# A gated mix of a Fourier layer and a Mish layer: the hand-ordered step list becomes a list of operations that a planner orders

## The chip, the cores and the metric

The kernel runs on one core of one Trainium2 chip. The metric is the device time of one execution in microseconds (us), the median of the runs shown; lower is better. The engines are TensorE (PE in the profile, PEld for its weight loads), VectorE (DVE), ScalarE (ACT), GpSimd (POOL) and SyncE (SP), which here issues nearly all DMAs. Each engine works through its own list in order.

## The reference

`x` is 2048 x 640 (S x D), and F is 1728. Two branches are mixed by a gate per row:

```python
g = sigmoid((x * gate_w).sum(-1, keepdims=True))
a, b = x @ Wd_re.T, x @ Wd_im.T                 # 640 x 640 each
y = Ws_re @ a - Ws_im @ b                       # 2048 x 2048 each
h = x @ w1 + b1
z = (h * tanh(softplus(h))) @ w2                # Mish; 640 x 1728 x 640
out = g * y + (1 - g) * z
```

All numbers are float32. The matrices of the Fourier branch are inputs; the kernel treats them as any matrices.

## The kernel before, in words

**Precision.** Every operand of a matmul is held as two numbers, a high part (the value copied to the type `fp32r`) and a low part (value less high part). A block product is three matmuls of 128 x 128 by 128 x 512: high x high, high x low, low x high (`mm3`). Making an operand (`split`, L82) costs one copy on ACT and one subtraction on DVE.

**Three products in turn.** The transposed result is made in three stages, of the kinds `seq` (the sequence products, with x as weights, kh = 8), `hid` (the hidden products, kh = 5) and `out` (the product with w2, kh = 6); the dense layer with w1 and Mish stands between hid and out. Intermediate tiles u (after seq), y (after hid) and act (after Mish) go to DRAM and are read back.

**Sums for products.** Within a stage a `Problem` treats two row tiles t1 and t2 of 512 columns and two halves of the inner dimension at once, by a scheme of the Strassen and Winograd kind: seven products in place of eight over four of the five 128-wide column blocks of the weights, on sums and differences of the operands. The fifth column block (block 5, columns 512 to 640) is multiplied plainly. A `Problem` has three parts: `first` (L302), which multiplies the top half a11 and leaves partial sums in banks a (two) and d1; `second` (L343) with the operands 22, 21, s2 = a21 + a22 - a11 and s1 = a21 + a22; `third` (L409) with 12, s3 = a11 - a21 and s4. Operand 21 serves only bank d2, block 5 of t2. PSUM has eight banks, all of them in use inside a Problem. Partial sums that must wait are copied to SBUF, or, for four Problems whose first part runs early (`aside`), to DRAM.

**Weights.** For each k the stage makes weight tiles with their two parts: `XA` (top block, block 5, one sum), `XB`, `XT13` and `XT2`. The 26 slots of pool W hold them; seq alone needs 26, hid 16. At the last Problem of a stage XA[k] is freed after s1 of k, in `second`; XB and XT13 after s4 of k, in `third`.

**The dense stage.** `dense_rest` (L673) makes the last two blocks of h for one t (25 matmuls). `dense_first` (L734) makes the other twelve, a pair fp and fp + 6 in eight steps: a11, s1, d2, s2, s4 + d1, s3, a12 + d1, a22 + d2, 54 matmuls in all, on four banks. Between uses of a bank a snapshot is taken: `snap` (L789) copies bank a after a11, bank b after s1, bank a after s2. `w1_job` (L605) makes the weights of one fp: two loads, four sums, six splits.

**Gate.** A job per t (`gate`, L885) multiplies tiles of the transposed x by columns of gate_w and adds them up on DVE, sums over partitions by two matmuls with ones, takes the sigmoid and stores g and 1 - g as full tiles. `gate_y` (L919) later loads each of the 20 tiles of y, multiplies it by g and stores it again. 1 - g is multiplied into the results of the first out Problem (`done`, `give`) and into act for t = 2, 3 (`out_act`, `act_q`).

**Order.** The program is a list of steps of matmuls. For each step, operands are made LEAD = 7 steps ahead (6 in the dense stage), loads are issued up to AHEAD = 9 beyond that while enough buffers are free, stores three steps later. Weights, gates and multiplications are jobs in a fixed list, started when a running estimate of DVE's clock (`clock["dve"]`) lies behind PE's by a set slack, and not in the steps `quiet` around the start of the dense stage. All loads and all stores but one go through SP in this order.

Of the kernel before, what the change touches and what calls it, by code (L numbers as in the profile page):

```python
# [13 lines left out]
P = 128  # L14
# [8 lines left out]
LEAD = 7  # L23
LEAD_D = 6
AHEAD = 9
SPARE, SPARE_D, SPARE_OUT = 3, 5, 4
SLACK, SLACK_UP = -1.0, 2.5
NR, NFS, NFX, NW, NL = 10, 20, 4, 26, 4
MM = 0.2267


class Slots:


    def __init__(self, items):
        self.free = list(items)

    def get(self):
        return self.free.pop(0)

    def put(self, *items):
        self.free.extend(items)
# [3 lines left out]
def fnet_mish_gate(ctx: ExitStack, tc: tile.TileContext, xn, xt, c_re, c_im, wd_re, wd_im,  # L46
# [7 lines left out]
    psum = Slots([pp.tile([P, N], F32, name=f"ps{i}") for i in range(8)])  # L54
    R = Slots([(sb.tile([P, N], F32R, name=f"rh{i}"), sb.tile([P, N], F32R, name=f"rl{i}")) for i in range(NR)])
    FS = Slots([sb.tile([P, N], F32, name=f"f{i}") for i in range(NFS)])
    FX = Slots([sb.tile([P, D], F32, name=f"fx{i}") for i in range(NFX)])
    W = Slots([(sb.tile([P, D], F32R, name=f"wh{i}"), sb.tile([P, D], F32R, name=f"wl{i}")) for i in range(NW)])
    ones = sb.tile([P, P], F32R, name="ones")
    b1s = sb.tile([P, NF], F32, name="b1s")  # L60
    gws = sb.tile([P, KD], F32, name="gws")

    def scratch(name, n, rows=P):
        return [[dr.tile([rows, N], F32, name=f"{name}{i}_{t}") for t in range(TG)] for i in range(n)]

    usc, ysc = scratch("u", 2 * KD), scratch("y", KD)
    gsc, qsc = scratch("g", 1)[0], scratch("q", 1)[0]
    asc = scratch("act", FC) + [[dr.tile([FR, N], F32, name=f"actr_{t}") for t in range(TG)]]

    clock = {"pe": 0.0, "dve": 0.0, "step": 0}  # L70
# [4 lines left out]
    def tt(o, a, b, op):  # L75
        clock["dve"] += 0.14 + 0.54 * a.shape[-1] / N
        nc.vector.tensor_tensor(o, a, b, op=op)  # L77

    def copy(o, a, scale=1.0):
        nc.scalar.activation(o, a, AF.Copy, scale=scale)  # L80

    def split(h, l, src):  # L82

        copy(h, src)
        tt(l, src, f32(h), OP.subtract)

    def mm(ps, a, b, start, stop):
        clock["pe"] += MM
        nc.tensor.matmul(ps, a, b, start=start, stop=stop, skip_group_check=True)  # L89

    def mm3(ps, ah, al, bh, bl, start, stop):
        mm(ps, ah, bh, start, False)
        mm(ps, ah, bl, False, False)
        mm(ps, al, bh, False, stop)

    def part(w, a, b):
        return w[0][:, a:b], w[1][:, a:b]

    def blocks(w, at, n):
        return [part(w, at + j * P, at + (j + 1) * P) for j in range(n)]  # L100

    A2, B2 = slice(0, 2 * P), slice(2 * P, 4 * P)

    RAW, XS, PS, OPS, KEEP, X, H = {}, {}, {}, {}, {}, {}, {}
    steps, stores, events, attach, narrow, takes = [], [], {}, [], set(), {}

    def at(i, fn):

        events.setdefault(i, []).append(fn)

    def step(raw, preps, mms, post=None):
        steps.append([list(raw), list(preps), mms, post])

    def store(dst, v, f):
        stores.append((dst, v, f, clock["step"] + (3 if clock["step"] < len(steps) - 8 else 0)))


    jobs, loaded, running, done_jobs = [], [], [], set()  # L120

    class Job:
        def __init__(self, key, work, load=lambda: [], w=0, fx=0, fs=0):
            self.key, self.work, self.load, self.w, self.fx, self.fs = key, work, load, w, fx, fs

    def simple(fn):
        def work(*a):
            fn(*a)
            return
            yield  # L130
        return work

    def fx_load(src, width=D):
        f = FX.get()
        nc.sync.dma_start(f if width == D else f[:, :width], src)
        return f

    def fs_load(src):
        f = FS.get()
        nc.sync.dma_start(f[:src.shape[0]], src)  # L140
        return f

    def job_load(i):
        j = jobs.pop(0)
        loaded.append((j, j.load(), i))

    def job_start():
        j, a, _ = loaded.pop(0)
        running.append((j.key, j.work(*a)))

    def job_go():
        key, work = running[0]
        pause = next(work, None)
        if pause is None:
            running.pop()
            done_jobs.add(key)
        return pause or 0

    def need(key):
        while key not in done_jobs:  # L160
            if not running:
                if not loaded:
                    job_load(0)
                job_start()
            job_go()

    class Stage:  # L170


        def __init__(self, kind, kh, row, neg=False):
            self.kind, self.kh, self.row, self.neg = kind, kh, row, neg
            self.XA, self.XB, self.XT13 = [None] * kh, [None] * kh, [None] * kh
            self.XT2 = [None] * (kh // KD + 1)

    def t2_part(st, k):
        return part(st.XT2[k // KD], k % KD * P, (k % KD + 1) * P)

    def b_sums(f, g):

        t = FS.get()
        tt(f[:, A2], f[:, B2], f[:, A2], OP.subtract)
        tt(f[:, B2], g[:, B2], f[:, B2], OP.subtract)
        tt(t[:, A2], g[:, B2], f[:, A2], OP.subtract)
        tt(t[:, B2], g[:, A2], t[:, A2], OP.subtract)
        return t

    def top(st, k, a, five):  # L190
        w = st.XA[k] = st.XA[k] or W.get()
        split(*part(w, 0, 2 * P), a)
        split(*part(w, 2 * P, 3 * P), five)

    def low(st, k, g, f):
        if st.neg:
            copy(g, g, -1.0)
            yield 1
        t = b_sums(f, g)
        yield 0  # L200
        w = st.XB[k] = W.get()
        st.XA[k] = st.XA[k] or W.get()
        st.XT13[k] = W.get()
        if k % KD == 0:
            st.XT2[k // KD] = W.get()
        split(*w, g)
        FX.put(g)
        yield 0
        split(*part(st.XA[k], 3 * P, 5 * P), t[:, B2])
        split(*part(st.XT13[k], 4 * P, 5 * P), t[:, :P])  # L210
        split(*t2_part(st, k), t[:, P:2 * P])
        FS.put(t)
        yield 0
        split(*part(st.XT13[k], 0, 4 * P), f)
        FS.put(f)

    tops = set()

    def stage_jobs(st, order):
        def do_top(k, g):  # L220
            top(st, k, g[:, A2], g[:, 4 * P:])
            FX.put(g)

        for what, k in order:
            if what == "top":
                jobs.append(Job((st.kind, "top", k), simple(lambda g, k=k: do_top(k, g)),
                                lambda k=k: [fx_load(st.row(k))], (st.kind, k) not in tops, 1))
            else:
                jobs.append(Job((st.kind, "low", k), lambda g, f, k=k: low(st, k, g, f),
                                lambda k=k: [fx_load(st.row(k + st.kh)), fs_load(st.row(k)[:, :4 * P])],  # L230
                                2 + (k % KD == 0) + ((st.kind, k) not in tops), 1, 1))
            tops.add((st.kind, k))

    def c_split(key, f):
        r = OPS[key] = R.get()
        split(r[0], r[1], f)
        FS.put(f)

    def op_done(key):
        R.put(OPS.pop(key))  # L240

    def product(name, stationary, key, first, last):

        if first and name not in PS:
            PS[name] = [psum.get() for _ in stationary]
        for ps, w in zip(PS[name], stationary):
            mm3(ps, *w, *OPS[key], first, last)

    def products_by_part(uses, key):

        h, l = OPS[key]
        todo = []
        for name, stationary in uses:
            PS[name] = [psum.get() for _ in stationary]
            todo += zip(PS[name], stationary)
        for n, c in ((0, h), (0, l), (1, h)):
            for ps, w in todo:
                mm(ps, w[n], c, n == 0 and c is h, False)

    def free_banks(name):  # L260
        psum.put(*PS.pop(name))

    def copy_out(name, keep=False):
        f = [FS.get() for _ in PS[name]]
        for ps, o in zip(PS[name], f):
            copy(o, ps)
            if not keep:
                psum.put(ps)
        if not keep:
            PS.pop(name)  # L270
        return f

    def add_out(name, f, keep=False):

        for ps, a in zip(PS[name], f):
            tt(a, ps, a, OP.add)
        if not keep:
            free_banks(name)
        return f
# [853 lines left out]
```

## Time and profile before

| | |
|---|---|
| median of 3 runs | 885.94 us (885.54 to 887.34) |
| span of the profiled execution, first to last instruction | 882.2 us |
| instructions | 12203 |
| PE, DVE, ACT busy, share of the span | 98%, 82%, 54% |
| matmuls | 3780 |
| DMA | 217.32 MB, 246 GB/s over the span |

The page prints the span of the profiled execution and no other time of it; the median of the runs is 3.7 us above that span. The rows of the profile quoted below are of this execution. A group of instructions is given by its line, engine, operation and operands, then "x" and the count, its busy time and the mean of one in ns. Overlapping instructions are counted once in the busy time, so that busy time over count is what one costs in a series, while the mean in ns is its full duration. In rows by stretches the columns after the stretch are its width, then busy time and (x count) of PE, PEld, DVE, ACT and POOL, the granted TensorE clock, the share of the DMA engines and GB/s. Rows of waits give total, times and the longest.

### The profile page before, as it was taken

Reading aid. Unit: us, or ns where it says so; the run is one execution under the profiler, and the core shown is the slowest. Engines: PE = TensorE matmul, PEld = TensorE weight load, DVE = VectorE, ACT = ScalarE, POOL = GpSimd, SP = SyncE. Lnnn points to the kernel's source line nnn. Section 1 sums busy time; section 2 is a strip of 40 time slices with the busy share of each in tenths; the row PEclk is TensorE's granted clock in tenths of the full one; section 3 lists DMA queues with packets and bytes.
Section 4 is the critical chain, followed back from the end, with each engine's and each line's share of the span. In section 5 each row is a group of like instructions: output and inputs, shape, how many; then the busy total and the mean of one; then the engine's idle time right before and its main releaser. Section 6 shows DMA issues by size and latency. Waiting matters only on the chain.

```text
span 882.2 us, 12203 instructions
## 1 busy us (share of the span) xinstructions
PE 864.0 (98%) x3780; PEld 710.4 (81%) x3780; DVE 724.2 (82%) x1262; ACT 477.5 (54%) x909; POOL 0.2 (0%) x4
## 2 busy tenths in 40 slices
PE   8999999999999999999999999899899999999998
PEld 6888888888888888888888888687688788888886
DVE  5999987899799668998997987663875889798994
ACT  6756545454565545647665667543644656442442
POOL 0000000000000000000000000000000000000000
PEclk9999999999999999999999999999999999999999
DMA  9975759596889664768767795489676777394952
GB/s 323 328 236 175 245 185 324 164 312 235 302 275 351 202 221 156 259 226 283 265 236 273 247 316 178 138 308 367 204 256 214 268 260 240 133 330 142 367 203 107
DMA packets 119392, 217.32 MB, mean 246 GB/s; under 512 B 13600, under 2 KB 16032, under 8 KB 119328
## 3 DMA queue, kind: packets, MB, share of 16 engines
q1 hardware_dynamic: 119184, 216.43, 71.6%
q8 instruction: 29, 0.48, 0.2%
q14 instruction: 35, 0.29, 0.1%
q10 hardware_dynamic: 144, 0.13, 0.0%
HBM read 170.11 MB, written 46.40 MB: 245 GB/s over the span
## 4 chain that ended last, share of the span: by engine, by line
PE 93%; DVE 3%; ACT 1%; DMA 1%; issue 1%; SPq 0%; DVEq 0%; ACTq 0%
PE ps L89 93%; DVE f L77 1%; DVE wl L77 1%; ACT wh L80 1%; DMA y<-f 1%; DVE rl L77 0%; DMA f<-in_xn_dram 0%; ACT f L671 0%; DMA act<-f 0%; DVE fx L77 0%; ACT f L80 0%; ACT rh L80 0%; SPq L1031 0%; SPq L1051 0%; DVE f L477 0%
## 5 line engine op out<-in xcount | busy, mean ns | idle before, releaser
L89 PE MATMUL ps<-rh,wh 128*128 128x512 f32 x1067 | 415.7, 390 | 7.4 <-ACT f L80 3.4
L89 PE MATMUL ps<-rh,wl 128*128 128x512 f32 x1053 | 409.4, 389 | 0.0
L89 PE MATMUL ps<-rl,wh 128*128 128x512 f32 x1052 | 409.1, 389 | 0.0
L80 ACT ACTIVATE rh<-f 128x512 fp32r<-128x512 f32 x413 | 243.7, 624 | 158.3 <-DVE f L77 103.9
L77 DVE TENSOR_TENSOR rl<-f,rh 128x512 fp32r<-128x512 f32 x411 | 267.0, 685 | 47.7 <-ACT rh L80 47.0
L89 PEld LDWEIGHTS ps<-rh,wh 128*128 128x128 f32 x1067 | 200.4, 188 | 52.7 <-ACT f L80 5.0
L89 PEld LDWEIGHTS ps<-rh,wl 128*128 128x128 f32 x1053 | 197.7, 188 | 40.9
L89 PEld LDWEIGHTS ps<-rl,wh 128*128 128x128 f32 x1052 | 197.4, 188 | 40.9 <-DVE rl L77 0.2
L77 DVE TENSOR_TENSOR f<-f,f 128x512 f32<-128x512 f32 x303 | 207.0, 689 | 19.2 <-DMA u<-f 6.3
L80 ACT ACTIVATE f<-ps 128x512 f32<-128x512 f32 (+1 forms) x146 | 84.9, 593 | 92.7 <-PE ps L89 74.7
L80 ACT ACTIVATE wh<-f 128x512 fp32r<-128x512 f32 (+2 forms) x158 | 68.9, 475 | 49.4 <-DVE f L77 40.4
L77 DVE TENSOR_TENSOR f<-ps,f 128x512 f32<-128x512 f32 x90 | 59.0, 685 | 35.1 <-PE ps L89 35.1
L77 DVE TENSOR_TENSOR wl<-f,wh 128x512 fp32r<-128x512 f32 (+2 forms) x157 | 73.8, 502 | 16.2 <-ACT wh L80 16.0
L89 PE MATMUL ps<-wh,wh 128*128 128x512 f32 x201 | 79.3, 395 | 5.4 <-ACT f L80 2.8
L89 PE MATMUL ps<-wl,wh 128*128 128x512 f32 x196 | 77.0, 393 | 0.0
L89 PE MATMUL ps<-wh,wl 128*128 128x512 f32 x195 | 76.6, 393 | 0.0
L77 DVE TENSOR_TENSOR wl<-fx,wh 128x640 fp32r<-128x640 f32 (+3 forms) x82 | 43.7, 554 | 11.6 <-ACT wh L80 11.6
L671 ACT ACTIVATE f<-f,b1s 128x512 f32<-128x512 f32 x36 | 25.9, 721 | 49.2 <-DVE f L77 49.2
L89 PEld LDWEIGHTS ps<-wh,wh 128*128 128x128 f32 x201 | 38.0, 189 | 15.4 <-ACT f L80 4.2
L80 ACT ACTIVATE wh<-fx 128x128 fp32r<-128x128 f32 (+5 forms) x83 | 40.6, 514 | 10.5 <-DMA fx<-in_xn_dram 3.5
L89 PEld LDWEIGHTS ps<-wh,wl 128*128 128x128 f32 x195 | 37.0, 190 | 7.8
L89 PEld LDWEIGHTS ps<-wl,wh 128*128 128x128 f32 x196 | 37.1, 189 | 7.5
(43 smaller groups left out, 177.3 us busy)
## 6 DMA issues: line engine op xcount, KB each, us to landing
f<-in_c_re_dram SPq DMA_DIRECT2D x128, 256.0 KB, 4.2
f<-in_c_im_dram SPq DMA_DIRECT2D x128, 256.0 KB, 4.1
f<-act SPq DMA_DIRECT2D x84, 256.0 KB, 5.2
f<-u SPq DMA_DIRECT2D x80, 256.0 KB, 4.6
f<-in_xt_dram SPq DMA_DIRECT2D x64, 256.0 KB, 4.6
act<-f SPq DMA_DIRECT2D x54, 256.0 KB, 4.5
u<-f SPq DMA_DIRECT2D x40, 256.0 KB, 3.5
y<-f SPq DMA_DIRECT2D x40, 256.0 KB, 4.5
```

Source lines behind the costliest of these rows:

```text
L77: nc.vector.tensor_tensor(o, a, b, op=op)
L80: nc.scalar.activation(o, a, AF.Copy, scale=scale)
L89: nc.tensor.matmul(ps, a, b, start=start, stop=stop, skip_group_check=True)
L671: nc.scalar.activation(o[rows], src[rows], AF.Mish, bias=b1s[rows, f:f + 1])
```

## The change

Nearly all of the kernel's body is rewritten. The same tilings, the same three stages and the same pools remain (R 10 operand pairs, W 26 weight pairs, 18 tiles F instead of 20, 6 tiles X instead of 4).

- **The order.** Operations are added to a `Graph` with their engine, an assumed duration and what they read and write. PE's list stays in the order written. `wants` works back from each matmul's place at 0.2267 us a matmul to when every other operation is wanted. `run` then plays all engines through with assumed durations, and each engine next emits, of the operations that are ready and whose buffers are granted, the one wanted first. A buffer is granted only if more are free than there are earlier wishes open for the same pool. Nothing here runs on the chip; it fixes the lists of instructions.
- **Block 5.** d2 starts from a copy of d1's sum after `first` (a11 times the top weights), and `third` adds s3, now a21 - a11, times the same weights. Operand 21 is gone. XA[k] is used until s3 of k in `third`.
- **Dense by turns.** `dense_first` treats two f alternately, step by step, with eight banks.
- **Gates from rows of x.** For each of 16 row tiles DVE multiplies x by gate_w, held in every partition, with a sum along the row (`accum_out`) into one column. g and 1 - g are stored as a row of 2048 through a transposing address pattern and loaded with the row repeated in all partitions. y is multiplied by g as it leaves hid; act at t = 2, 3 by 1 - g as it leaves Mish.
- **Start.** Warming uses two memsets of 128 x 512 in place of one of 128 x 128 and one of 128 x 512; the two wide loads of block 5 of x take their place by their wants.

```diff
+    def wants(self):
+        for op in self.ops:
...
+            if op.engine == "PE":
+                op.ends = op.at + op.took
+                op.want = op.at
+                continue
+            op.prompt = op.psum or not op.fills and any(d.prompt and d.engine in ("ACT", "DVE") for d in op.deps)
+            if op.prompt:
+                op.ends = max([d.ends for d in op.deps if d.prompt or d.engine == "PE"], default=0) + op.took
+                op.want = op.ends + (PROMPT if op.psum else LATER)
+        for op in reversed(self.ops):
+            late = min([a.want for a in op.after], default=1e9) - op.took - HOP
+            op.want = late if op.want is None else min(op.want, late)
...
+                    p, n = v.pool, bisect_left(v.pool.asks, v.ask)
+                    if not op.prompt:
+                        n += bisect_left(p.soon, (v.ask[0] + AHEAD,)) - bisect_left(p.soon, v.ask)
+                    if len(p.free) <= n:
+                        blocked.add(v.pool)
+                        return False
...
+    def dve(emit, r, w, n=N, more=0.0):
+        took = 0.15 + n / 960 + more
+        return G.add("DVE", emit, r, w, took, took - 0.083)
+    def act(emit, r, w, n=N, more=0.0):
+        took = 0.21 + n / 1260 + more
+        return G.add("ACT", emit, r, w, took, took - 0.096)
+    def dma(queue, emit, r, w, size):
+        return G.add(queue, emit, r, w, 1.95 + size / 385e3, 0.605 if queue == "SP" else 1.0)
...
+    class Problem:
+        def first(self, top):
...
+            self.p1, self.d = [to_sbuf(b) for b in self.a], to_sbuf(self.d1)
...
+        def second(self, low):
...
+            d2 = self.d
...
+            self.d2 = copy(bank(), d2)
...
-            for p, k in in_turn(kh, ("22", "21", "s2", "s1"), ("22", "21", "s2", "s1"), ("22", "21", "s2", "s1")):
+            for p, k in in_turn(kh, *[("22", "s2", "s1")] * 3):
...
+                if p == "22":
+                    product(p4, st.blocks("t4", k), x, k == 0 and not opened, k == kh - 1)
+                    product([self.d2], st.blocks("low5", k), x, False, k == kh - 1)
...
+        def third(self):
...
+                    tt(a21, a21, a11, OP.subtract)
+                    tt(a22, a22, a21, OP.add)
+                    tt(a22, a12, a22, OP.subtract)
...
+                elif p == "s3":
+                    product(self.a, st.blocks("t3", k), x, False, end)
+                    product([self.d2], st.blocks("five", k), x, False, end)
...
+        def done(self, b, d, t):
+            f = Val(FS)
+            if self.q:
+                tt(f, b, self.q(t), OP.mult)
+            else:
+                copy(f, b)
+            self.plus(f, d, t)
+        def give(self, d, t, f):
+            if self.q:
+                tt(f, f, self.q(t), OP.mult)
+            self.plus(f, d, t)
...
+    def broadcast(row, t):
+        return load(FS, lambda: row.t[:, t * N:(t + 1) * N].partition_broadcast(P), row)
...
+        for f0 in range(0, FP, 2):
+            pair_ = (f0, f0 + 1)
+            for f in pair_:
+                w1_block(f)
...
+            for f in pair_:
+                times(bk[f][0], "a11", [(w[f][0], k) for k in range(2)], True, True)
+                p1[f] = to_sbuf(bk[f][0])
+            for f in pair_:
+                times(bk[f][1], "s1", [(w[f][2], k) for k in range(2)], True, True)
+                p5[f] = to_sbuf(bk[f][1])
+            for f in pair_:
+                times(bk[f][3], "d2", [(w[f][1], 4)], True, True)
+            for f in pair_:
+                times(bk[f][0], "s2", [(w[f][2], 4), (T2B[f // KD], f % KD)], False, True)
+                u2[f] = to_sbuf(bk[f][0])
...
+    def gates():
+        wide = load(X, gw.partition_broadcast(P), cols=D)
+        for k in range(KS):
+            x = load(X, xn[k], cols=D)
+            dve(lambda k=k, x=x: nc.vector.scalar_tensor_tensor(
+                x.t, x.t, 1.0, wide.t, op0=OP.mult, op1=OP.mult, accum_out=gcol.t[:, k:k + 1]),
+                whole(x, wide), whole(x) + [(gcol, k)], D, 0.1)
...
+        for c, row, r in ((gcol, grow, cols), (qcol, qrow, whole(qcol))):
+            dma("SP", lambda c=c, row=row: nc.sync.dma_start(row.t.rearrange("o (k p) -> p (o k)", p=P), c.t),
+                r, whole(row), 1 << 18)
...
     for q in range(4):
         if q == 3:
-            sq[3].first()
-        sq[q].second()
+            sq[3].first(seq_top)
+        sq[q].second(seq.low)
+        if q == 2:
+            gates()
         sq[q].third()
```

More of the change, by code (lines that the diff above doesn't have):

```diff
@@ L79, in copy @@
-    def copy(o, a, scale=1.0):
[L80 to L97, printed above, removed]
@@ L138, in fs_load @@
[L138 to L165, printed above, removed]
@@ L234, in c_split @@
[L234 to L258, printed above, removed]
@@ new lines, in tt, with fresh, to_sbuf @@
+    def tt(o, a, b, op, cut=(slice(None),) * 3, rows=slice(None), n=N):
+        (x, y, z) = cut
+        dve(lambda: nc.vector.tensor_tensor(o.t[rows, x], a.t[rows, y], b.t[rows, z], op=op),
+            whole(a, b), whole(o), n)
+    def fresh(pool, a, b, op):
+        o = Val(pool)
+        tt(o, a, b, op)
+        return o
+    def copy(o, a, scale=1.0):
+        act(lambda: nc.scalar.activation(o.t, a.t, AF.Copy, scale=scale), whole(a), whole(o))
+        return o
+    def to_sbuf(bank):
+        return copy(Val(FS), bank)
@@ new lines, in fnet_mish_gate, with keep, raw, mish @@
+    once = {}
+    def keep(key, make):
+        if key not in once:
+            once[key] = make()
+        return once[key]
+    def broadcast(row, t):
+        return load(FS, lambda: row.t[:, t * N:(t + 1) * N].partition_broadcast(P), row)
+    def raw(t, k):
+        return load(FS, xt[t, k])
+    def mish(o, src, f, rows=slice(0, P), bias=True):
+        more = dict(bias=b1s.t[rows, f:f + 1]) if bias else {}
+        act(lambda: nc.scalar.activation(o.t[rows], src.t[rows], AF.Mish, **more),
+            whole(src, table) + whole(b1s) * bias, whole(o), more=0.1)
@@ L1088, in fnet_mish_gate @@
-    for dst, v, f, _ in stores:
-        nc.sync.dma_start(dst, v)
-        FS.put(f)
+    hd[0].first(hid.top)
+    hd[1].first(hid.top)
+    for p in hd:
+        p.second(hid.low)
+        p.third()
+    for t in (2, 3):
+        dense_rest(t, [operand(raw(t, k)) for k in range(KD)])
+    have = {}
+    for t, names in ((0, ("a11", "a11", "a12", "a12", "d1")), (1, ("a21", "a21", "a22", "a22", "d2"))):
+        xs = [operand(raw(t, k), W if n in ("a11", "a12", "a22") else R) for k, n in enumerate(names)]
+        for k, n in enumerate(names):
+            if n != "a21":
+                have[n, k % 2 if k < 4 else 0] = xs[k]
+        dense_rest(t, xs)
@@ L1093 @@
+    dense_first(0, have)
+    dense_first(1, {})
+    ou[0].first(fin.top)
+    ou[1].first(fin.top)
+    for p in ou:
+        p.second(fin.low)
+        p.third()
+    G.run([psum, R, FS, X, W], 385.0, 1.95)
 def kernel(**inputs):
```

1307 lines of the change are left out of this document (519 added, 788 removed).

## The prediction

> **What bounds the kernel now.** First the page: who is busy, and at which TensorE clock.
>
> ```profile
> PE 864.0 (98%) x3780; PEld 710.4 (81%) x3780; DVE 724.2 (82%) x1262; ACT 477.5 (54%) x909; POOL 0.2 (0%) x4
> ...
> PEclk9999999999999999999999999999999999999999
> ```
>
> TensorE is the bound, so a change pays only where it takes matmuls away or fills gaps between them. Second, the chain that ended last, in order of time, gives the price of a matmul in unbroken flow.
>
> ```profile
> 7.40 547.11 PE ps L89 x2412
> ```
>
> 547.11 / 2412 = 0.2268 us. Third, the table by stretches: one row for the flow, four where it breaks, one for the tail.
>
> ```profile
> 7.40:554.50 547.10, 547.10 (x2413) 453.02 (x2414) 472.36 (x818) 320.14 (x608) 0.00 (x0) 1.00 0.74 252
> 554.50:572.90 18.40, 14.97 (x64) 11.26 (x63) 14.18 (x34) 10.54 (x27) 0.00 (x0) 1.00 0.51 154
> 611.10:630.10 19.00, 13.62 (x50) 9.78 (x48) 11.01 (x19) 9.15 (x17) 0.00 (x0) 0.91 0.81 272
> 684.20:692.40 8.20, 7.42 (x33) 5.82 (x31) 6.18 (x14) 4.45 (x9) 0.00 (x0) 1.00 0.62 211
> 700.90:706.30 5.40, 4.19 (x20) 2.98 (x18) 5.33 (x12) 3.22 (x6) 0.00 (x0) 1.00 0.66 214
> 878.30:882.20 3.90, 0.14 (x1) 0.00 (x0) 0.42 (x1) 0.38 (x1) 0.00 (x0) 1.00 0.38 134
> ```
>
> The span of 882.2 divides into 7.4 before the first real matmul, 3772 matmuls (3780 less 8 for warming) x 0.2268 = 855.5, the tail of 3.9, and what is left: 15.4 us of waiting. Width less count x 0.2268 finds 3.9, 7.7, 0.7 and 0.9 of it in the four broken stretches, all in the dense stage; the row of 611 also shows a granted clock of 0.91 around the longest gap. Fourth, the waits say for what.
>
> ```profile
> PE ps L89 <- ACT f L80: 6.2, 5, 2.4
> PE ps L89 <- DVE f L77: 4.6, 4, 1.4
> PE ps L89 <- ACT rh L80: 2.0, 1, 2.0
> ```
>
> and, of the window from 554 to 707 alone, for all engines:
>
> ```profile
> ACT f L80 <- DMA y<-f: 4.6, 1, 4.6
> ```
>
> The matmul waits for a bank to be copied out (the snapshots of `dense_first`) or added out; at 611 that copy itself waited for a buffer whose store of y had not landed. Of PE's own waits only the 2.0 at the start lie outside the dense stage.
>
> **The change, part by part.** Matmuls: each stage keeps 18 block products per k (first 3; second 8 becomes 7, third 7 becomes 8), `dense_first` 18, the rests 25 matmuls each. Only the gate's two matmuls per t go, 8 in all: 8 x 0.2268 = -1.8.
>
> Start. Now two wide loads are issued ahead of the first tiles.
>
> ```profile
> 0.72 1.00 SPq L1031 DMA_DIRECT2D fx<-in_xn_dram  x2
> 0.82 0.17 DVE L938 MEMSET ones<- 128x128 f32 x1 [0.82 <-PEq L1121]
> 1.04 0.48 DVE L940 MEMSET rh<- 128x512 f32 x1
> ...
> 1.58 3.78 PE L89 MATMUL ps<-rh,ones 128*128 128x512 f32 x8 [1.58 <-DVE rh L940]
> ...
> 2.30 0.43 SPq L1051 DMA_DIRECT2D f<-in_xn_dram  x1
> ...
> 6.21 0.42 ACT L80 ACTIVATE wh<-f 128x256 fp32r<-128x256 f32 x1 [4.20 <-DMA f<-in_xn_dram]
> ...
> 7.40 0.96 PE L89 MATMUL ps<-rh,wh 128*128 128x512 f32 x3 [2.03 <-ACT rh L80]
> ```
>
> By wants, the c tile goes first, then the x tile, then one wide load; the second wide load is wanted only at k=5. The x tile is issued some 1.1 us sooner with two wide loads fewer ahead of it, but the second memset (0.48 for 0.17) moves the warming matmuls 0.3 later, to end near 5.7. The first real matmul lies between 5.7 and 7.4; the third still needs the wide load, so I take 6.0: -1.4 (ends -1.7 and 0).
>
> Block 5. The operand "21" goes: 4 x 8 + 2 x 5 + 2 x 6 = 54 splits, each one copy on ACT and one subtraction on DVE. In exchange each problem copies d1 out and preloads d2 (16 ACT copies at most).
>
> ```profile
> L77 DVE TENSOR_TENSOR rl<-f,rh 128x512 fp32r<-128x512 f32 x411 | 267.0, 685 | 47.7 <-ACT rh L80 47.0
> L80 ACT ACTIVATE rh<-f 128x512 fp32r<-128x512 f32 x411 | 242.6, 624 | 157.6 <-DVE f L77 103.9 <-PE ps L89 39.8 <-DMA f<-act 4.9
> L77 DVE TENSOR_TENSOR f<-f,f 128x512 f32<-128x512 f32 x301 | 205.8, 689 | 19.2 <-DMA u<-f 6.3 <-DMA y<-f 2.9 <-DMA f<-act 1.8
> ...
> L80 ACT ACTIVATE ps<-f 128x512 f32<-128x512 f32 x26 | 14.5, 596 | 1.9 <-DVE f L77 1.9
> ...
> L894 DVE SCALAR_TENSOR_TENSOR f<-f,gws,f 128x512 f32<-128x512 f32 x16 | 11.9, 745 | 0.0
> ```
>
> Back to back a split holds DVE 267.0 / 411 = 0.65, so 54 x 0.65 = -35 on DVE; on ACT 54 x 0.59 = -32, +10. None of it is on the path: in the sequence stage the flow is unbroken at 86% DVE (472.36 of 547.10). It is room, not time. One path appears: in `sq[3]` first runs straight into second, and d2's preload waits for d1's copy, 2 x 0.596 behind the last d1 matmul, against six p4 matmuls, 1.36: 0 to 0.8, I take 0.3. And XA[k] now lives until third's s3 (it was freed in second), so hid's weights can be made only while `sq[3].third` releases W. Hid begins after 8 x 4 x 54 + 8 matmuls, at 7.4 + 1736 x 0.2268 = 401.2, and that part, 8 x 24 matmuls, 43.6 earlier, at 357.6; its price is in the stretch counted below.
>
> Gates and multiplications. The gate over columns (16 + 4 multiplications, 4 splits) becomes 16 row operations of 640; from 745 ns at 512 columns I scale 745 + 128 x 0.6 / 0.512 ns, about 0.9, so 16 x 0.9 = 14 on DVE. y is multiplied as it leaves hid: 20 DVE operations move out of the dense and out stages into hid, 12 of them in place of ACT copies, and the stores and loads behind the wait at 611 vanish:
>
> ```profile
> y<-f SPq DMA_DIRECT2D x40, 256.0 KB, 4.5
> f<-y SPq DMA_DIRECT2D x39, 256.0 KB, 4.9
> ...
> b1s<-in_b1a_dram SPq DMA_DIRECT2D x1, 6.5 KB, 2.4
> b1s<-in_b1b_dram SPq DMA_DIRECT2D x1, 0.2 KB, 2.6
> ```
>
> Some 40 transfers fewer pass SP, which still takes all loads and stores in one list: a store that waits for a late DVE result holds the loads behind it. Four multiplications with 1-gate move from a later job to the dense rests, 4 x 0.65 = 2.6 beside matmuls. The new stores of gate and 1-gate are 2048 pieces of 4 bytes each. No row has that. Below: 2.4, as 128 small pieces (6.5 KB) land no later than 64 (2.6). Above: if all of 2.4 grew with the pieces, 16 x 2.4 = 38. I take 5 each, nearer the first, since twice the pieces added nothing; covered, as the planner starts the chain before hid's first multiplication.
>
> [...]
>
> Dense by turns. One f at a time gives a snapshot only the one step between two uses of a bank: `s1` (6 matmuls) and `d2` (3), about 2.0, before s2 reopens bank a, with ACT busy. With two f alternating, s2 of the first f comes after a11 of the second, 2 s1 and 2 d2, 1.36 + 2.7 + 1.36 = 5.4 later; s3 waits 4.1 after u2, a22 5.4 after s3. A copy and an addition cost 0.6 and 0.69, so the four breaks go: -13.2, and with the rest of the 15.4 up to -15.4. What is late next: both f's weights (W1) must be ready at once.
>
> The order. Whether every gap closes depends on DVE, which the planner must fill in the stretch before and around the dense entry. The rows:
>
> ```profile
> 357.60:401.20 43.60, 43.60 (x194) 36.13 (x193) 39.79 (x70) 25.80 (x50) 0.00 (x0) 1.00 0.72 249
> 401.20:523.70 122.50, 122.50 (x543) 101.45 (x542) 111.84 (x198) 78.96 (x155) 0.00 (x0) 1.00 0.78 266
> 421.60:445.40 23.80, 23.80 (x107) 19.71 (x106) 22.41 (x41) 16.48 (x33) 0.00 (x0) 1.00 0.81 275
> 546.40:707.40 161.00, 150.16 (x644) 120.56 (x643) 109.00 (x205) 82.09 (x160) 0.00 (x0) 0.99 0.72 245
> ```
>
> The first two are `sq[3].third` and hid: 151.6 of 166.1 us of DVE, 91%, without a break. Changes: -10 hid splits x 0.65 = -6.5; +20 multiplications x 0.65 = +13; gates +14, which fall here because their six X buffers are asked for after hid's 20 (5 top, 15 low) and those wait for W. Sum 172, 6 more than the stretch holds. Against it: up to ten operands (R holds 10) already made at 357, 10 x 0.65 = 6.5, and weight work for dense that can slip into the dense stage, where the last row has DVE 109.0 busy of 161.
>
> So DVE is nearly full for 170 us and PE will wait somewhere between hid's middle and the second pair. Bounds: 0 if everything slips, 14 if the gates fit nowhere. I take 4, as 6 excess against 6.5 in hand nearly cancel, but even the fullest part of hid ran DVE at 94% (22.41 of 23.80).
>
> Sum: 882.2 - 1.8 - 1.4 - 15.4 + 0.3 + 4 = 867.9 of span. The page gives only the span; the median of the runs, 885.94, is 3.7 above it, so 871.6 as a time.
>
> **The rivals.**
> *DVE bound in hid.* The accumulating row operation is in no trace; the plain form with the same two tensors ran 745 ns for 512 columns. If an accumulator halves its pace, each takes about 0.9 + 0.67, and the 14 becomes 25. With 6 + 11 - 6.5 = 10 uncovered the time is 882.2 + 3.7 - 18.6 + 0.3 + 10 to 14: 878 to 882. For it: the 91% above. Against: the row of 745. [...]
>
> *Late gates (the other side).* The first multiplication by the gate's row stands in DVE's order after s3 of hid's first problem, 285 matmuls into hid, near 465. If its row is late, all operand splits behind it stand, and PE runs dry after the operands in hand, some 5 us. The stores delay the queue too. With s per store the row comes 2 x (s - 2.7) later than planned (the planner takes 1.95 + 0.68 + 0.1). The gain of 14.3 is used up when 2(s - 2.7) - 5 exceeds it, about s = 12.5. At s = 20, midway between the bounds, the loss is 30 and the time 902 or, with the clock slowed after such a gap as at 611, some 2 more; at 38 it is 937. For it: that no row shows such writes; against: 128 pieces at 2.4. [...]
>
> *The order does no better.* DMA landed in 4.5 to 4.9 where the planner counts 2.6 plus its queue; if every transfer is late and the dense breaks return in new places, only -3.2 stays: 882.7. Against: the flow held 547 us unbroken with these landings.
>
> **How the numbers follow.** About 0.2% (1.8 us) is what a measurement can tell from no change. Forecast, stalls of 0 to 8 left: 867 to 876, chance 0.58. DVE bound, 876 to 884: 0.17. No better order, 881 to 887: 0.07, half of it within 0.2%. Late gates, 886 and above: 0.18, of which 0.01 within 0.2%. The range runs from 867, the sum with no stall left, to 887, leaving out most of the late-gate case. Faster: 0.58 + 0.17 + 0.035 = 0.785, rounded to 0.79; same 0.04; slower 0.17.
>
> **What would show it.** Matmuls 3772; first real one near 6.0; the windows of the dense stage at width = count x 0.2268; no f<-y before the out stage but 20; DVE operations about 50 fewer, DVE share over 95% from 360 to 560. It is wrong if PE waits for ps or rh near 430 to 470 for more than 8 us, if the gate's row operation takes over 1.2 us, or if grow's store lands after more than 12.

## The result: 0.24% slower, and one place in the trace

The changed kernel takes 888.3 us (median of 19 runs, 887.33 to 890.98) against 886.0 us (19 runs, 883.74 to 888.07): a ratio of 1.0024, 95% interval 1.0017 to 1.0032. The profiled execution spans 886.2 us, 2.1 below the median. The forecast was 871.6; the measured time lies above it and above its range.

The page of the changed kernel, the engines' busy times and TensorE's granted clock:

```profile
PE 862.9 (97%) x3772; PEld 711.6 (80%) x3772; DVE 677.5 (76%) x1213; ACT 461.7 (52%) x849; POOL 0.2 (0%) x4
...
PEclk9999999999999999999997899999999999999999
```

All the work that was to go has gone: 8 matmuls, 49 operations of DVE with 47 us, 60 of ACT, some 14 MB of transfers. New is a dip of the clock near the middle, to 7 and 8 tenths in two slices. The table by stretches (width, then busy time and count of PE, PEld, DVE, ACT, POOL, clock, DMA share, GB/s) cuts the span where TensorE's flow breaks:

```profile
0.00:5.76 5.76, 3.77 (x9) 3.00 (x10) 2.00 (x4) 2.25 (x4) 0.20 (x4) 1.00 0.56 166
5.76:470.73 464.97, 464.47 (x2044) 383.68 (x2042) 367.68 (x658) 249.53 (x459) 0.00 (x0) 1.00 0.71 242
470.73:492.81 22.08, 6.76 (x18) 5.13 (x17) 16.42 (x30) 5.88 (x10) 0.00 (x0) 0.61 0.63 187
492.81:816.53 323.72, 323.72 (x1430) 267.96 (x1428) 242.55 (x444) 176.98 (x331) 0.00 (x0) 1.00 0.63 215
816.53:827.42 10.89, 9.29 (x38) 6.66 (x37) 7.92 (x13) 4.63 (x9) 0.00 (x0) 1.00 1.06 387
827.42:882.30 54.88, 54.88 (x243) 45.14 (x241) 40.51 (x67) 22.05 (x38) 0.00 (x0) 1.00 0.58 205
882.30:886.20 3.90, 0.04 (x1) 0.00 (x0) 0.42 (x1) 0.38 (x1) 0.00 (x0) 0.85 0.38 134
```

Width less count x 0.2268 gives 1.4 us lost in the second row, 18.0 in the third, 2.3 in the fifth, and nothing in the 324 us of the fourth, which holds the whole dense stage. Before, 15.4 us were lost, 13.2 of them in the dense stage. So the change closed what it was to close and opened one gap of 18.0 us, between hid's first problem and its second. Without it the span would be 868.2; the prediction's sum was 867.9. How far that nearness is luck is said further below.

The chain that ended last, in order of time, names what filled the gap (start, us, what):

```profile
449.66 11.21 DMA grow<-gcol
...
464.25 12.73 DMA f<-u
...
486.31 312.58 PE ps L292 x1365
```

and SP's list around it shows the order of the transfers (start, time that SP was held, what):

```profile
449.66 0.37 SPq L753 DMA_DIRECT2D grow<-gcol  x1
450.07 2.58 SPq L246 DMA_DIRECT2D f<-ph  x1
460.96 0.80 SPq L246 DMA_DIRECT2D f<-grow  x2
461.80 1.92 SPq L246 DMA_DIRECT2D f<-u  x2
463.82 0.38 SPq L753 DMA_DIRECT2D qrow<-qcol  x1
464.25 2.76 SPq L246 DMA_DIRECT2D f<-u  x1
```

The store of g (`grow`, 2048 pieces of 4 bytes) lands after 11.2 us. The load that repeats this row must wait for it, at the head of SP's list, so that SP issues nothing from 452.7 to 461.0. SP's own wait in this window:

```profile
SPq L246 <- DMA grow<-gcol: 8.2, 1, 8.2
```

Then loads of u go out, and behind them the store of 1 - g; the next load of u lands 12.7 us after its issue, where the median of all loads of u is 5.4. In steps of 5 us, with the same columns as above:

```profile
450.00:455.00 5.00, 5.00 (x24) 4.14 (x23) 5.00 (x9) 4.59 (x8) 0.00 (x0) 1.00 0.64 127
455.00:460.00 5.00, 5.00 (x24) 4.14 (x23) 3.88 (x8) 0.40 (x1) 0.00 (x0) 1.00 0.59 37
460.00:465.00 5.00, 5.00 (x24) 4.14 (x23) 0.00 (x0) 0.00 (x0) 0.00 (x0) 1.00 0.64 155
465.00:470.00 5.00, 5.00 (x24) 4.14 (x23) 0.96 (x2) 0.63 (x1) 0.00 (x0) 1.00 0.58 80
470.00:475.00 5.00, 1.00 (x5) 0.50 (x3) 1.34 (x4) 0.00 (x0) 0.00 (x0) 1.00 0.68 41
475.00:480.00 5.00, 0.00 (x0) 0.00 (x0) 3.00 (x6) 0.68 (x2) 0.00 (x0) 0.54 0.90 315
480.00:485.00 5.00, 0.00 (x0) 0.00 (x0) 5.00 (x10) 3.36 (x6) 0.00 (x0) 0.50 0.02 7
485.00:490.00 5.00, 3.69 (x9) 2.94 (x10) 5.00 (x9) 1.21 (x3) 0.00 (x0) 0.50 0.85 287
```

Behind each store the rate falls, to 37 and 41 GB/s, while the share of the DMA engines stays at 0.59 and 0.68; behind the first, SP's stopped list is part of the reason. DVE runs out of work at 459, some twelve microseconds before TensorE does: the operands in hand carried PE from 459 to 471. Then PE stands 15.3 us, and when it starts its clock is at 0.50 (the row of 485).

The chain also shows that the wait does not end with the load. The load of u lands at 477.0 and PE goes on at 486.3: for these 9.3 us DVE works through what had piled up in its list behind the sum of u that waited: more sums and operand parts for the second problem, and then the additions and multiplications by g that empty the first problem's banks, for which PE waits.

### The profile page after: what moved, and what is told of

Same layout as the page of the kernel before. It is cut to its first block, busy times and chain, and to the rows that moved or that the text cites. A ratio compares the mean times of both kernels' runs of the same rounds, so it can differ in the third digit from the quotient of the medians.

```text
span 886.2 us, 11840 instructions
## 1 busy us (share of the span) xinstructions
PE 862.9 (97%) x3772; PEld 711.6 (80%) x3772; DVE 677.5 (76%) x1213; ACT 461.7 (52%) x849; POOL 0.2 (0%) x4
## 4 chain that ended last, share of the span: by engine, by line
PE 85%; DMA 7%; DVE 5%; ACT 1%; issue 1%; SPq 1%; DVEq 0%; ACTq 0%
PE ps L292 85%; DMA f<-u 3%; DVE f L259 2%; DMA grow<-gcol 1%; DMA x<-in_xn_dram 1%; DVE x L746 1%; DMA f<-act 1%; DMA ph<-f 1%; DVE x L259 0%; PE ps L715 0%; SPq L246 0%; ACT f L268 0%; DMA out_dram<-f 0%; DVE r1l L287 0%; DVE r8l L287 0%
## 5 line engine op out<-in xcount | busy, mean ns | idle before, releaser
L268 ACT ACTIVATE f<-ps 128x512 f32<-128x512 f32 x129 | 74.8, 594 | 41.1 <-PE ps L292 35.0
L286 ACT ACTIVATE r8h<-f 128x512 fp32r<-128x512 f32 x42 | 26.4, 628 | 26.0 <-DVE f L259 13.6
L287 DVE TENSOR_TENSOR r7l<-f,r7h 128x512 fp32r<-128x512 f32 x39 | 26.8, 687 | 13.3 <-ACT r7h L286 13.1
L286 ACT ACTIVATE r0h<-f 128x512 fp32r<-128x512 f32 x40 | 25.2, 629 | 20.1 <-PE ps L292 10.9
L287 DVE TENSOR_TENSOR r4l<-f,r4h 128x512 fp32r<-128x512 f32 x40 | 27.5, 688 | 10.2 <-ACT r4h L286 10.2
L287 DVE TENSOR_TENSOR r2l<-f,r2h 128x512 fp32r<-128x512 f32 x41 | 28.2, 687 | 9.3 <-ACT r2h L286 9.2
L287 DVE TENSOR_TENSOR r1l<-f,r1h 128x512 fp32r<-128x512 f32 x41 | 28.2, 688 | 9.0 <-ACT r1h L286 8.8
L287 DVE TENSOR_TENSOR r8l<-f,r8h 128x512 fp32r<-128x512 f32 x42 | 28.8, 687 | 7.7 <-ACT r8h L286 7.4
L287 DVE TENSOR_TENSOR r5l<-f,r5h 128x512 fp32r<-128x512 f32 x40 | 27.5, 687 | 9.3 <-ACT r5h L286 9.3
L287 DVE TENSOR_TENSOR r0l<-f,r0h 128x512 fp32r<-128x512 f32 x40 | 27.5, 687 | 9.2 <-ACT r0h L286 9.1
L287 DVE TENSOR_TENSOR r6l<-f,r6h 128x512 fp32r<-128x512 f32 x40 | 27.5, 687 | 7.0 <-ACT r6h L286 6.7
```

The lines of the kernel that those rows point to most:

```text
L268: act(lambda: nc.scalar.activation(o.t, a.t, AF.Copy, scale=scale), whole(a), whole(o))
L286: act(lambda: nc.scalar.activation(r.t[0][:, :N], src.t[:, :N], AF.Copy), whole(src), [(r, 0)])
L287: dve(lambda: nc.vector.tensor_tensor(r.t[1][:, :N], src.t[:, :N], f32(r.t[0][:, :N]), op=OP.subtract), whole(src) + [(r, 0)], [(r, 1)])
```

## The experiments

### The two stores in pieces of 64 bytes

Theory A: the two stores hold the loads. Theory B: DVE is too full in this stretch, and the stores are bystanders. Row tile k of the gate becomes rows 16 p + k, so that a partition's 16 results are neighbours in the row.

```diff
+        rows = xn.rearrange("k p d -> (k p) d").rearrange("(p k) d -> k p d", k=KS)
...
-            x = load(X, xn[k], cols=D)
+            x = load(X, rows[k], cols=D)
...
-            dma("SP", lambda c=c, row=row: nc.sync.dma_start(row.t.rearrange("o (k p) -> p (o k)", p=P), c.t),
+            dma("SP", lambda c=c, row=row: nc.sync.dma_start(row.t.rearrange("o (p k) -> p (o k)", p=P), c.t),
```

> The changed kernel with one edit: row tile k of the gate is rows 16 p + k of x instead of 128 k + p, so that the 16 columns of a partition are neighbours in the row and g and 1 - g are stored as 128 pieces of 64 bytes instead of 2048 of 4 bytes. The planned order of all instructions stays the same. Theory A (the two stores of 4-byte pieces hold up all loads behind them, and the first also holds SP's list, since the load of the repeated row waits at its head): the stores land in 2.4 to 4 us instead of 11, the gap of TensorE at 471 to 493 goes with its 18 us, time 888.3 - 18 = 870 (868 to 873). Theory B (DVE is too full in this stretch, as feared in the prediction; the stores only come at the same time): a gap of 10 us or more stays there, time 880 or above.

Measured: 873.46 us, a ratio of 0.9851 to the kernel before (0.9826 to 0.9875), a little above the 868 to 873 that was expected. The landings of the two stores (min/median/max, us) and the stretches from 440 to 530, where the flow breaks three times:

```profile
DMA to landing us min/median/max: 3.8/4.1/4.5
```

```profile
440.00:448.00 8.00, 7.34 (x33) 5.76 (x32) 8.00 (x16) 6.09 (x13) 0.00 (x0) 1.00 1.02 370
448.00:470.70 22.70, 22.70 (x102) 18.80 (x101) 21.36 (x41) 11.92 (x22) 0.00 (x0) 1.00 0.55 183
470.70:475.00 4.30, 3.54 (x17) 2.63 (x16) 4.30 (x8) 1.12 (x2) 0.00 (x0) 1.00 0.86 300
475.00:525.00 50.00, 50.00 (x222) 41.42 (x221) 46.96 (x88) 29.35 (x61) 0.00 (x0) 1.00 0.77 267
525.00:530.00 5.00, 3.75 (x17) 2.75 (x16) 5.00 (x9) 0.63 (x1) 0.00 (x0) 1.00 0.97 329
```

The gap is gone and with it 14.8 us (by the ratios to the kernel before, 1.0024 and 0.9851, 15.3). Theory A holds. What of theory B is true is small: by idle PE (width less busy) 0.7, 0.8 and 1.3 us remain in this stretch, where DVE is busy without a pause, 2.7 together where the prediction set 4. Another 1.5 us are idle at 800 to 805, in the stage out. The edit also changes which rows the gate's loads fetch; the next two runs leave the loads as they are.

### One store at a time

The same edit of the store's address for 1 - g alone, and then for g alone. The gate's loads stay as in the changed kernel, so each of these kernels stores one row in another order than it is read and leaves out the right factor of one branch; its work and its order of operations stay.

> The changed kernel with only the second store (1 - g) in 64-byte pieces; g keeps its 2048 pieces. 1 - g is then stored in a wrong arrangement, so it leaves out the right factor of the second branch; the work and the order are the same. Theory A: DVE still idles some 10 us behind the first store (459 to 469 in the changed kernel), but the loads after it land in 5 us instead of 12, so TensorE, which had operands until 471, loses 0 to 5 us: 870 to 875. If the cost of the stores were simply additive, half of 18 us would stay: 879. Theory B: above 880.

> The changed kernel with only the first store (g) in 64-byte pieces; 1 - g keeps its 2048 pieces, and g is stored in a wrong arrangement, so it leaves out the right factor of the first branch. Theory A: SP is no longer stopped at the load of the repeated row; the second store goes out some 8 us sooner and holds the loads behind it about 11 us, about what TensorE has in hand: it loses 0 to 5 us, time 870 to 875. Additive cost: 879. Theory B: above 880.

Measured: 882.25 us (ratio 0.9941, 0.9922 to 0.9961) and 881.03 us (0.9927, 0.9904 to 0.9950). Each store in small pieces costs by itself about 8 us over the 873.46 of the run without (8.8 for g, 7.6 for 1 - g); I had expected the operands in hand to cover one of them, and the additive guess came nearer. Both miss the expected 870 to 875. TensorE's longest wait in each of the two:

```profile
PE ps L292 <- DVE f L259: 10.2, 1, 10.2
```

```profile
PE ps L292 <- DVE f L259: 7.5, 1, 7.5
```

In the second nothing at SP's head waits for the small pieces, and still PE waits 7.5 us: the hold of the loads suffices. Whether the stopped list adds to it is not shown, as the intervals of the two times overlap. Nor did any run send the two stores through another engine's queue.

### The same stores early

```diff
+        self.prompt, self.ends, self.want, self.psum, self.due = False, 0.0, None, False, 1e9
...
+            op.want = min(op.due, late if op.want is None else min(op.want, late))
...
-                r, whole(row), 1 << 18)
+                r, whole(row), 1 << 18).due = 200.0
```

> The changed kernel with the two stores of 4-byte pieces kept, but wanted at 200 us of the planner's time instead of about 450, so that the 16 row operations and the stores fall into the sequence stage, where DVE has room and nothing on SP waits for the rows. Theory A in its strong form (any 11 us hold of the loads costs time): two gaps of 3 to 8 us near 200, time 875 to 885. Theory A in its weak form (the hold costs only where DVE has no operands in hand and SP is stopped as well): hidden, 869 to 873. Theory B: hid's DVE has 14 us less to do, and the gap goes too: 869 to 873; so against B it is e1 that decides, and this run says whether the pieces cost anything when they come early.

Measured: 881.4 us (0.9930, 0.9906 to 0.9955), so the weak form falls. The stores go out at 151.4 and 152.1, back to back, and land after 15.8 and 17.7 us; the loads behind them come to 61 and 33 GB/s for 12 us:

```profile
148.00:154.00 6.00, 6.00 (x28) 4.99 (x27) 5.41 (x10) 2.39 (x6) 0.00 (x0) 1.00 1.06 397
154.00:160.00 6.00, 6.00 (x29) 4.95 (x28) 4.26 (x7) 1.13 (x3) 0.00 (x0) 1.00 0.87 61
160.00:166.00 6.00, 6.00 (x28) 4.99 (x27) 0.00 (x0) 0.00 (x0) 0.00 (x0) 1.00 1.03 33
166.00:172.00 6.00, 2.54 (x12) 1.77 (x10) 0.00 (x0) 0.00 (x0) 0.00 (x0) 0.93 0.65 77
```

Even where DVE had room, what TensorE had in hand did not outlast this double hold. Beside 870.51 for the same early gate with 64-byte stores (further below), the small pieces cost 10.9 us here.

### What makes the pieces slow

Six transfers of a 128 x 16 tile, used by nobody, put into the kernel before, each some 45 us from the next.

```diff
+            (70, lambda: nc.sync.dma_start(col(rows[0], KS), probe.rearrange("p (k w) -> p k w", w=1))),
+            (100, lambda: nc.sync.dma_start(col(rows[1], KS // 2), probe[:, :KS // 2].rearrange("p (k w) -> p k w", w=1))),
+            (130, lambda: nc.sync.dma_start(col(rows[2], KS // 2, 2), probe.rearrange("p (k w) -> p k w", w=2))),
+            (160, lambda: nc.sync.dma_start(rows[3].rearrange("o (p k) -> p (o k)", p=P), probe)),
+            (190, lambda: nc.sync.dma_start(wide[:, :1].rearrange("(k p) w -> p k w", p=P), probe.rearrange("p (k w) -> p k w", w=1))),
+            (220, lambda: nc.sync.dma_start(got.rearrange("p (k w) -> p k w", w=1), col(rows[0], KS)))):
```

> The kernel before with six extra transfers of a small tile, each alone in the sequence stage some 45 us apart and used by nobody: (1) 2048 pieces of 4 bytes into one row of 8 KB, as in the changed kernel; (2) 1024 pieces of 4 bytes; (3) 1024 pieces of 8 bytes; (4) 128 pieces of 64 bytes; (5) 2048 pieces of 4 bytes, each 512 bytes from the next; (6) a load of 2048 pieces of 4 bytes. Theory A1 (each small write costs a fixed time): landings of about 11, 6.5, 6.5, 2.4, 11 us. Theory A2 (the writes collide because neighbours share a small block of memory): (5) lands in 5 or less, or (3) in much less than (2). The load (6): 3 to 5 if only writes are slow, 11 if pieces are slow either way. TensorE loses up to 8 us behind (1) and (5), as behind the early stores of the last call.

Measured, each once, from issue to landing: (1) 2048 pieces of 4 bytes as neighbours in 8 KB: 12.4 us; (2) 1024 such pieces in 4 KB: 10.3; (3) 1024 pieces of 8 bytes in 8 KB: 5.7; (4) 128 pieces of 64 bytes: 4.5; (5) 2048 pieces of 4 bytes, each 512 bytes from the next: 5.5; (6) the load of 2048 pieces: 3.6. The answers for (1) and (5):

```profile
DMA to landing us min/median/max: 12.4/12.4/12.4
```

```profile
DMA to landing us min/median/max: 5.5/5.5/5.5
```

The number of pieces is not the cost (1 against 5, 2 against 3), nor are small reads (6). What is slow here (12.4 and 10.3 us) is pieces of 4 bytes that lie next to each other and come from different partitions. That is theory A2 as far as it was put to the test; why such writes are slow together, and whether they share a block of memory, no run shows. The whole run took 885.79 us, one execution, beside 886.04 for the kernel before. The loss of up to 8 us behind (1) and (5) did not come: in the 15 us from the issue of (1) on, 119 to 134, TensorE is busy throughout. So one such hold, in the sequence stage of the hand-ordered list, cost next to nothing; the losses above came from one hold between hid's two problems, or from two in a row.

### Block 5 undone

With 64-byte stores, operand 21 is made again.

```diff
-            d2 = self.d
-            if y:
-                d2 = y(4, t2)
-                tt(d2, d2, self.d, OP.add)
-            self.d2 = copy(bank(), d2)
+            self.d2 = copy(bank(), y(4, t2)) if y else bank()
...
+                elif p == "21":
+                    product([self.d2], st.blocks("five", k), x, False, k == kh - 1)
...
-                    product([self.d2], st.blocks("five", k), x, False, end)
```

> The kernel with 64-byte stores, with block 5 as before the change: operand 21 is made again (54 splits: 35 us on DVE, 32 on ACT) and d2 no longer starts from the first row's partial sum. As predicted (room, not time): 872 to 876. Rival (DVE is so full between hid's start and the dense pairs, 93% there, that hid's ten splits of 6.5 us are paid in full or more): 879 to 884.

Measured: 869.26 us (0.9813, 0.9798 to 0.9828), by medians 4.2 us faster than with the new block 5, though DVE and ACT do 54 splits more; the ratios differ by 3.4 us, and their intervals just touch. Neither theory had that. The gap at 318, where d2 waits for a copy of a copy, is gone, as are those at 443 and 526; the 1.5 us at 800 to 805 shrink to 0.1, and 1.3 us remain near 475. A later pair tells how much is block 5's own.

### One f at a time in the dense stage

```diff
-        for f0 in range(0, FP, 2):
-            pair_ = (f0, f0 + 1)
+        for f0 in range(FP):
+            pair_ = (f0,)
```

> The kernel with 64-byte stores, with the dense stage one f at a time instead of two by turns. As predicted (the turns close the breaks): each step now waits for the snapshots of its bank again, and the kernel loses 5 to 13 us: 878 to 886. Rival (the planner's order alone closes them): 872 to 875.

Measured: 877.39 us (0.9897, 0.9879 to 0.9915), 3.9 us slower than with two by turns. So the turns bring about 4 us, less than the 5 to 13 expected. The rest of the 13.2 us of dense breaks must be closed by other parts of the rewriting; the planner's order and the stores of y that are gone are two candidates, which no run separates.

### The gate early, with 64-byte stores

The edit `due = 200.0` from above, on the kernel with 64-byte stores.

> The kernel with 64-byte stores, with the gate's stores wanted at 200 us of the planner's time, so that the gate's 16 row operations (14 us on DVE) and loads (5 MB) leave the full stretch of hid for the sequence stage. If the small gaps left at 443, 471 and 526 (3.1 us together) are DVE's and the loads' crowding there: 870 to 872. If they are set by the order of banks: 873 to 874.

Measured: 870.51 us (0.9825, 0.9810 to 0.9840). The three gaps at 443, 471 and 526 are gone in the trace: they came from the gate's work and loads, which were crowded into hid. By medians that is 3.0 us; the intervals of the two ratios overlap.

### The fastest version, and block 5 once more

> 64-byte stores, operand 21 made again, and the gate's stores wanted at 200 us: the two edits that helped, together. If they remove different gaps (the early gates those at 443, 471 and 526; operand 21 also the one at 318, where d2 waits for a copy of d1, and part of those near 800): 866 to 868. If both only relieve the same crowded stretch of hid: 869 to 870.

> 64-byte stores and operand 21 made again, with the planner's fixed part of a transfer raised from 1.95 to 2.8 us, nearer the landings of 4 to 5 seen. If late transfers, which the planner thinks shorter, cause the small gaps left (475, 565, 800): 867 to 868. If not: 869 to 871.

The second of these also has the early gate, which its expectation does not say: it is the first with 2.8 in place of 1.95 in `dma` and in the call of `run`. Measured: 867.59 us (0.9784, 0.9770 to 0.9799) and 865.99 us (0.9766, 0.9750 to 0.9782). The two edits remove different gaps, and a planner that counts transfers longer removes another 1.6 us. The last one's flow, from its start to its tail:

```profile
9.40:860.40 851.00, 851.00 (x3754) 704.41 (x3753) 703.48 (x1254) 486.27 (x884) 0.00 (x0) 1.00 0.70 236
```

In this stretch nothing is left to gain by order: 851.00 / 3754 = 0.2267 us a matmul.

> The same three edits as the fastest kernel so far (64-byte stores, gate wanted at 200 us, fixed part of a transfer at 2.8 us in the planner), but with block 5 as the change has it (d2 from the first row's partial, no operand 21). It differs from the run with 865.99 us in block 5 alone. If block 5's new form costs time by itself (d2 waits for two copies in a row at 318; its chain of s3 and the later release of XA near 800): 868 to 870. If its loss of 4.2 and 2.9 us in the earlier pairs was only the planner's thin margin for transfers: 866 to 867.

Measured: 867.91 us (0.9791, 0.9773 to 0.9809). By medians block 5's new form costs 1.9 us with everything else as in the fastest version. The two intervals overlap a little, but the trace shows where 1.2 of it lie: TensorE idles 0.3 us at 318, 0.7 at 798 and 0.15 at 806, where the other does not. These waits of TensorE

```profile
PE ps L713 <- DVE r9l L711: 2.0, 1, 2.0
PE ps L292 <- ACT w1h L280: 0.3, 1, 0.3
```

are those of the version with 865.99, and with the new block 5:

```profile
PE ps L292 <- DVE r6l L287: 0.7, 1, 0.7
PE ps L715 <- DVE r9l L713: 2.0, 1, 2.0
PE ps L292 <- ACT ps L268: 0.3, 1, 0.3
PE ps L292 <- ACT w0h L280: 0.3, 1, 0.3
```

The wait for `ACT ps` is d2's copy. The same pair with 64-byte stores differed by 4.2 us, with the gate early by 2.9 (870.51 against 867.59); why the difference shrinks with each edit is not shown.

### The changed kernel with operand 21 alone

The edit of "Block 5 undone" with the small pieces kept.

> The changed kernel with only operand 21 made again; the stores stay at 2048 pieces of 4 bytes. If the loss behind the stores comes from the stores and not from block 5: the gap of 15 us and the slowed clock after it stay, 883 to 889. If block 5's later release of the weights is what leaves TensorE too little in hand to cover the stores: 870 to 880.

Measured: 879.41 us (0.9917, 0.9902 to 0.9932), inside the second range, which made block 5 share in the loss. The four medians stand in a square: the small pieces cost 14.8 us with the new block 5 (888.30 against 873.46) and 10.2 with operand 21 (879.41 against 869.26); the new block 5 costs 8.9 us with small pieces and 4.2 without. So the stores are most of the loss, and the new block 5 makes it larger. How it does so is open. Here the first store goes out 20 us sooner, at 429.6, and lands in 12.0, and PE's longest wait behind it is 4.4 us; the second, at 467.1, meets operands in hand. That points to where the stores fall, but the later release of the weights, which the expectation named, changed in the same edit.

## Why the prediction was wrong, step by step

**The step that failed** is in the part on gates: "I take 5 each, nearer the first ... covered, as the planner starts the chain before hid's first multiplication." The two stores took 11.2 and 11.1 us, and neither was covered. The bounds (2.4 to 38) held; the value was chosen by rows whose pieces are loads, and loads of small pieces turned out quick (3.6) where such writes are not. The sum put nothing at all for them; they cost 18.0 us of span, 14.8 by the run without small pieces.

The late-gate rival described the event: its place (near 465, found 471), its two holds, the slowed clock. It was given 0.18, too little for a price that no row bounded well. Its arithmetic, 2 x (11.2 - 2.7) - 5 + 2 = 14, gives 871.6 + 14 = 886; measured 888.3. That this comes so near is partly luck. It took some 5 us of operands in hand, and PE ran on for 12; it left out the 9.3 us that DVE needs after the load has landed. And it is not the multiplication that waits first but a sum of u tiles, whose loads stand behind the stores.

Luck is also in the 868.2 that remain without the gap, against a sum of 867.9. Outside the gap the sum's 4 us of waiting between hid's middle and the dense pairs hardly appear in the changed kernel; in their place 2.3 us are lost at 816 to 827, in the stage out, which no term had, and the start won 0.5 less than was taken. The 3.7 us that the sum adds to the span to get the time were 2.1 here.

A price by the size of a piece alone would not have held either: among the six probes pieces of 4 bytes took 12.4 us as neighbours and 5.5 us at a distance of 512 bytes.

**Matmuls**, -1.8: right, 3772.

**Start**, -1.4: the first real matmul came at 5.6 where 6.0 was taken, but the first ones were slow. The rows of the changed kernel's start (start, us, engine):

```profile
5.56 1.48 PE L292 MATMUL ps<-r0h,w0h 128*128 128x512 f32 x3
6.84 1.31 PE L292 MATMUL ps<-r0l,w0h 128*128 128x512 f32 x3
```

The first matmuls start 0.43 us apart, as they do at the clock of 0.50 behind the long gap, though the clock column reads 1.00 here; why is not shown. The seventh real matmul starts at 7.99, and at 8.92 in the kernel before: the size was off, -0.9 in place of -1.4.

**Dense by turns and order**, -15.4: right as a sum (the fourth stretch has no loss), but wrong in its parts: the turns were to bring 13.2 and carry only 3.9.

**Block 5**, "room, not time", +0.3: d2's copy cost 0.3 at 318, as forecast, but the new form costs some 2 us in all in the best version, 4.2 in the kernel with 64-byte stores. The room on DVE was not needed: the fastest version runs DVE 703.5 us of 851.

**DVE nearly full**, 4 taken: 2.7 measured in the run with 64-byte stores, at the three places between hid's middle and the dense pairs, and gone when the gate work is put early. The gate's 16 operations came where they were expected, in hid, from 415 on. Their time, 14, was right:

```profile
L746 DVE SCALAR_TENSOR_TENSOR x<-x,x x16: 816/819/826, 415.4 to 447.2; 128x640 f32<-128x640 f32 x16
L746 DVE DVE_READ_ACCUMULATOR x<-x,x x16: 80/82/85, 416.2 to 447.9; 128x1 f32 x16
```

819 + 82 ns for 640 columns is no slower a pace than the 745 ns for 512 of the form without a sum; the rival that the accumulator halves it falls.

**The order does no better**: fell. With 64-byte stores the rewritten kernel is faster than the hand-ordered one by 1.5%, in its best version by 2.3%.

## What to carry to other kernels

A store whose neighbours of 4 bytes come from different partitions is not small because its bytes are few: here it took 11.2 us, and the loads behind it waited with it (12.7 for a load of u, median 5.4). So arrange the computation so that each partition writes one piece of 64 bytes, here by taking rows 16 p + k in place of 128 k + p: these stores took 3.8 and 4.5 us. When a price is in no row, ask first whether the rows that bound it go in the same direction (loads or stores), and let the bad end of a wide bound weigh more than a guess that the time is covered, above all when other work stands behind it in an in-order list. A planner's list is only as good as its worst-known duration: here two stores, each counted at 2.7 us and taking 11, undid a gain of some 14.

## What the runs showed of the hardware

Small writes to neighbouring addresses were slow together, not one by one: 2048 pieces of 4 bytes took 12.4 us as neighbours and 5.5 us at a distance of 512 bytes; 1024 pieces took 10.3 at 4 bytes and 5.7 at 8. Loads issued after them were held with them, though they go to other addresses: a load of u landed after 12.7 us (median 5.4), and behind the two early stores the rate was 33 to 77 GB/s for 18 us. A load of 2048 pieces of 4 bytes took 3.6 us. After the 15.3 us in which TensorE stood, its clock was at 0.50 for about the first 6 us of work, which cost some 2.7 us more than the wait itself (18.0 us lost in that stretch).
